# P read in place in 64-query blocks on TensorE column tiles, with V copied by halves, in a fused attention and gMLP block

## The chip, the cores and the metric

The kernel runs on one core of one Trainium2 chip. The metric is device time in microseconds (us); lower is better. A core has five engines with instruction queues of their own: TensorE (PE in the profile, with its weight loads listed apart as PEld), VectorE (DVE), ScalarE (ACT), GpSimd (POOL) and SyncE (SP), which issues most DMAs. Engines wait for each other through semaphores; within an engine instructions run in the order in which they were written.

## The reference

One token sequence of 2048 rows and 448 columns goes through two sub-blocks. Both are modulated by six vectors `mod = silu(c) @ w_mod`.

```python
h = layernorm(x) * (1 + ca) + sa
q, k, v = split(h @ wqkv)                      # 16 heads of 28
scores = q @ k.T * 28 ** -0.5
scores = where(0 <= i_query - i_key < 256, scores, -1e9)
x = x + ga * (softmax(scores) @ v) @ wo        # sliding window of 256

h = layernorm(x) * (1 + cb) + sb
z = gelu(h @ w_in)                             # 1792 columns
g = w_sp @ layernorm(z[:, 896:]) + b_sp        # w_sp mixes the 2048 rows
x = x + gb * (z[:, :896] * g) @ w_out
```

## The kernel before, in words

The rows are cut into 16 tiles of 128 and four blocks of 512. All work is entered as operations in a small planner (`Sched`, with one `add` for each). A long string, `ORDER`, lists operation numbers with the engine that takes each and the PSUM or SBUF slot that it gets: that string is the written order of every engine's queue. The semaphore waits follow from the dependencies. On an engine, an operation that waits holds up everything listed behind it.

*Head.* x, `w_mod`, and the query, key and value weights are loaded. The narrow products of `mod_cols` (L535, L540) turn c into the modulation columns; L540 writes a second copy into the upper 64 partitions, on the second column tile of the array. Statistics come from `stats` (L592 to L600), the normalised rows from `norm` (L609 to L620), the transposes from PE (L666) for the first two blocks and from DMA for the others. Q and K are projected by blocks of 512 rows (L696 for the first four groups of block 0, L708 for the others, L743 for the keys of the last block), V by tiles (L756), with 32 columns for each head: 28 values, a one that sums up P, and three unused (`Vaug`).

*Attention.* A query tile sees up to three key blocks of 128: the oldest (partly masked), the middle one (whole) and its own (partly masked). Each query tile is worked in two halves of eight heads. For tiles 0 and 1 L832 makes the scores. For tiles 2 to 15 L858 makes them with matmuls of 32 rows of the array (four heads side by side on four row tiles) into four PSUM banks, packed so that the oldest and the own block share columns: 36 matmuls for each half, the last 16 of them with 64 stationary columns on two column tiles. L867 adds the middle block of the other four heads by one product of 512 columns with a block-diagonal copy of Q (`QBD`, made by DMA at L734). ACT exponentiates 2048 and 512 columns (L819) into `PW`. DVE multiplies the packed part with the mask (L874, two products of 1024 columns for each half) and writes it, spread out again, into a second buffer `PT`. L901 is P·V: the stationary operand is a 128x128 block of P (128 keys, 128 queries), the moving operand 32 columns of `Vaug`; three key blocks and eight heads make 24 matmuls for each half. DVE divides by the sums (L915, L917), a DMA transposes the result (`oT`), L926 multiplies with `wo`, L931 adds x.

*Second half.* Statistics and a DMA transpose again (`hT2`), L951 modulates, L1011 and L1032 make z, ACT applies gelu (L1018, L1040), DVE normalises the second half of z (L592, L1023). L1055 is the spatial product (448 matmuls of 512 columns, with `w_sp` transposed by DMA), L1059 and L1062 add the bias and multiply, L1072 multiplies with `w_out`, L1082 adds x and SP writes the tile out.

The functions that the change touches and what calls them:

## Time and profile before

| | us |
|---|---|
| median of 3 runs | 280.3 (280.0 to 280.85) |
| the profiled execution's own time | 279.08 |
| its span, first to last instruction | 277.4 |

| engine | busy us | share of the span | instructions |
|---|---|---|---|
| PE | 266.4 | 96% | 3198 |
| PEld | 140.8 | 51% | 3225 |
| DVE | 164.4 | 59% | 364 |
| ACT | 128.2 | 46% | 154 |
| POOL | 127.2 | 46% | 191 |

The granted TensorE clock was 1.0 all through. The shares are means over stages of different kinds: in the attention stage DVE, ACT and PE are all close to full, in the last 118 us PE alone works and the others follow it. A matmul's length in the table includes its way through the array, and matmuls overlap: how fast they follow each other is read from their starts, not from their lengths. A row of the waits names who waited, for whom, the sum, the number of waits and the longest.

### The profile page before, as it was taken

How to read it: one execution, taken by the hardware profiler on the slowest of the kernel's cores; microseconds unless marked ns; L12 is line 12 of the kernel's file. 1: busy time of each engine (PE TensorE's matmuls, PEld its weight loads, DVE VectorE, ACT ScalarE, POOL GpSimd, SP SyncE). 2: the span in 40 equal slices, each digit the busy share in tenths (PEclk: the TensorE clock that was granted, in tenths of full speed). 3: DMA queues.
4: the chain of work that ended last, by engine and by line, in shares of the span. 5: the costliest groups of instructions: out<-in, count | busy, mean ns of one | idle time of the engine just before them, and what ended most of it. 6: DMA issues, size and time to landing. Idle time of an engine off the chain costs nothing.

```text
span 277.4 us, 7383 instructions
## 1 busy us (share of the span) xinstructions
PE 266.4 (96%) x3198; PEld 140.8 (51%) x3225; DVE 164.4 (59%) x364; ACT 128.2 (46%) x154; POOL 127.2 (46%) x191
## 2 busy tenths in 40 slices
PE   4999999999999999999999999999999999999995
PEld 1636466656576766444444444444444444444452
DVE  5679999989989999679798300300320042025434
ACT  2587999999999999577676600000000000000000
POOL 6831826914725669884949000600571065334110
PEclk9999999999999999999999999999999999999999
DMA  7966142145993666834999999100000000001113
GB/s 208 304 170 205 23 91 47 21 80 96 121 225 79 80 80 97 194 77 83 190 176 205 206 197 187 35 0 0 0 2 0 0 0 2 0 0 56 62 50 99
DMA packets 65843, 26.01 MB, mean 94 GB/s; under 512 B 56466, under 2 KB 64723, under 8 KB 65811
## 3 DMA queue, kind: packets, MB, share of 16 engines
q1 hardware_dynamic: 65168, 24.68, 43.4%
q10 hardware_dynamic: 642, 0.86, 1.1%
q8 instruction: 25, 0.41, 0.6%
q14 instruction: 8, 0.06, 0.1%
HBM read 9.01 MB, written 1.84 MB: 39 GB/s over the span
## 4 chain that ended last, share of the span: by engine, by line
PE 82%; DVE 8%; DMA 4%; POOL 3%; issue 1%; ACT 0%; ACTq 0%; SPq 0%; POOLq 0%
PE ps L1055 35%; PE ps L1032 8%; PE ps L1072 7%; PE ps L1011 6%; PE ps L708 5%; PE ps L901 5%; PE ps L858 3%; DMA hT<-xn 3%; PE ps L926 3%; PE ps L756 3%; PE ps L867 2%; DVE st_all L592 2%; PE ps L557 1%; DMA c_row<-in_c_dram 1%; PE ps L696 1%; POOL hT L951 1%
## 5 line engine op out<-in xcount | busy, mean ns | idle before, releaser
L819 ACT ACTIVATE PW<-ps 128x2048 bf16<-128x2048 f32 (+1 forms) x56 | 67.4, 1242 | 2.9 <-PE ps L867 1.1
L1059 DVE TENSOR_TENSOR tmpg<-ps,bsp_bc 128x512 bf16<-128x512 f32 x28 | 19.1, 691 | 83.4 <-PE ps L1055 69.3
L1062 POOL TENSOR_TENSOR z1T<-tmpg,z1T 128x512 bf16<-128x512 bf16 x28 | 31.9, 1153 | 79.3 <-DVE tmpg L1059 79.3
L1055 PE MATMUL ps<-wspB,z 128*128 128x512 bf16 x218 | 49.5, 379 | 0.3
L1055 PE MATMUL ps<-wspA,z 128*128 128x512 bf16 x220 | 48.8, 379 | 0.3 <-issue 0.2
L874 DVE TENSOR_TENSOR PT<-PW,mask 128x1024 bf16<-128x1024 bf16 x56 | 38.9, 721 | 0.7 <-ACT PW L819 0.7
L1055 PEld LDWEIGHTS ps<-wspA,z 128*128 128x128 bf16 x224 | 21.8, 98 | 26.6 <-issue 0.4
L1055 PEld LDWEIGHTS ps<-wspB,z 128*128 128x128 bf16 x224 | 21.9, 98 | 26.2
L600 POOL TENSOR_TENSOR rs_all<-ve_all,neghalf 128x1 f32<-128x1 f32 (+2 forms) x37 | 23.6, 645 | 3.7 <-DVE ve_all L597 3.0
L1011 PE MATMUL ps<-w_in,hT 64*128 64x448 bf16 x224 | 23.0, 349 | 1.2 <-DVE hT L951 0.6
L901 PE MATMUL ps<-Vaug,PT 128*128 128x32 bf16 x496 | 24.1, 177 | 0.1
L901 PEld LDWEIGHTS ps<-Vaug,PT 128*128 128x128 bf16 x496 | 21.8, 96 | 4.0 <-DVE PT L894 0.6
L1032 PE MATMUL ps<-hT,w_in 64*128 64x512 bf16 x196 | 22.5, 376 | 0.0
L1072 PE MATMUL ps<-w_out_g,z1T 128*128 128x448 bf16 x112 | 22.2, 352 | 0.0
L708 PE MATMUL ps<-hT,WQK 128*128 128x512 bf16 x80 | 20.5, 379 | 1.3 <-issue 0.4
L616 POOL TENSOR_SCALAR xn<-x_sb,rs_all,ve_all 128x448 bf16<-128x448 bf16 x21 | 18.1, 863 | 7.0 <-DMA hT<-xn 6.4
L901 PE MATMUL ps<-Vaug,PW 128*128 128x32 bf16 x224 | 20.1, 176 | 0.0
L592 DVE BATCH_NORM_STATS2 st_all<-x_sb 128x6 f32<-128x448 bf16 x32 | 18.9, 610 | 1.6 <-DMA x_sb<-in_A_x_dram 1.5
L592 DVE BATCH_NORM_STATS2 st_all<-z 128x6 f32<-128x448 bf16 x32 | 18.3, 607 | 1.7 <-ACT z L1018 1.7
L901 PEld LDWEIGHTS ps<-Vaug,PW 128*128 128x128 bf16 x224 | 17.6, 96 | 1.9
L597 POOL TENSOR_SCALAR ve_all<-mv_all 128x1 f32<-128x1 f32 (+2 forms) x20 | 6.6, 334 | 25.1 <-DVE mv_all L595 21.5
L1018 ACT ACTIVATE z<-ps 128x896 bf16<-128x896 f32 x16 | 14.1, 916 | 7.8 <-PE ps L1011 6.8
(101 smaller groups left out, 343.9 us busy)
## 6 DMA issues: line engine op xcount, KB each, us to landing
out_dram<-fin SPq DMA_DIRECT2D x16, 112.0 KB, 1.7
x_sb<-in_A_x_dram SPq DMA_DIRECT2D x3, 448.0 KB, 3.9
wmod<-in_w_mod_dram SPq DMA_DIRECT2D x1, 1344.0 KB, 9.5
w_in<-in_B_w_in_dram SPq DMA_DIRECT2D x1, 1344.0 KB, 8.2
QBD<-qT SPq DMA_DIRECT2D x16, 64.0 KB, 2.5
w_out_g<-in_B_w_out_dram SPq DMA_DIRECT2D x1, 784.0 KB, 4.9
bsp_bc<-in_B_b_sp_dram SPq DMA_DIRECT2D x1, 512.0 KB, 5.0
x_sb<-in_A_x_dram SPq DMA_DIRECT2D x2, 224.0 KB, 4.2
```

The source lines that it names most:

```text
L592: st = [dve(0.62 if True else 0, lambda e, t=t, ci=ci, s=s: e.bn_stats(st_all[:, slot, t, ci, :], s()), deps(t), prio) for ci, s in enumer ...
L600: rs = pool(0.53 + 0.15 * len(tiles), lambda e: e.tensor_tensor(rs_all[:, slot, a:b], ve_all[:, slot, a:b], neghalf[:, 0:b - a], ALU.pow), ...
L708: m = pe(4 * MMS, [lambda e, h=h, g=g, kc=kc, tb=tb: e.matmul(ps[:, h.slot[0], :], lhsT=WQK[:, kc, 4 * g:4 * g + 4, :].rearrange("p a b -> ...
L819: ex = act(xdur, lambda e, out_ap=out_ap, in_ap=in_ap: e.activation(out_ap(), in_ap(), ACT.Exp, scale=SCALE), [s], v - 8.0 + u, takes, tab ...
L874: return dve(0.70, lambda e: e.tensor_tensor(cols(hp.slot[0] * 2048 + 1024 * k, [[256, 4], [128, 2], [1, 128]]), cols(at_w() + 128 + 192 * ...
L901: fns.append(lambda e, hp=hp, hO=hO, hi=hi, bi=bi, kb=kb, hd=hd, nb=nb, a=at[hi][bi], p_of=p_of: e.matmul(ps[:, hO.slot[0], 32 * hd:32 * h ...
L1011: return lambda e, kc, p0, start, stop: e.matmul(ps[:, hs[t % 2].slot[hf], 0:D], lhsT=hT[p0:p0 + 64, kc, t * 128:(t + 1) * 128], rhs=w_in[ ...
L1032: return lambda e, kc, p0, start, stop: e.matmul(ps[:, hs[b // 2].slot[b % 2], :], lhsT=w_in[p0:p0 + 64, kc, ft * 128:(ft + 1) * 128], rhs ...
L1055: m = pe(16 * MMS, [lambda e, h=h, si=si, ft=ft, tb=tb: e.matmul(ps[:, h.slot[0], :], lhsT=z2[:, si, ft * 128:(ft + 1) * 128], rhs=(wspA i ...
L1059: a = dve(0.7, lambda e, h=h, ht=ht, tb=tb: e.tensor_tensor(tmpg[:, ht.slot[0], :], ps[:, h.slot[0], :], bsp_bc[:, tb * 512:(tb + 1) * 512 ...
L1062: u = pool(1.16, lambda e, ht=ht, ft=ft, tb=tb: e.tensor_tensor(z1T[tb][:, ft, :], tmpg[:, ht.slot[0], :], z1T[tb][:, ft, :], ALU.mult), [ ...
L1072: return [lambda e, ft=ft: e.matmul(ps[:, h.slot[0], 0:D], lhsT=z1T[t // 4][:, ft, (t % 4) * 128:(t % 4 + 1) * 128], rhs=w_out_g[:, ft, :] ...
```

## The change

- **P·V.** P stays where the exponential wrote it (`PW`). For each head there are six products in place of three: the stationary operand is 64 queries wide, and the products of the first and of the last 64 queries go to the two column tiles of the array (`tile_position=(0, 0)` and `(0, 64)`). The packed columns now hold, in one 128-key column block, keys of the own block beside keys of the oldest, so V must be packed alike: `VX` holds four versions of V (two of them with the other half of the keys zero), made by two copies and four DMAs for each block of four tiles (`V_half`, `vdma` below); `VX` has two buffers and its zeros are set early.
- **Scores.** 40 matmuls for each half, all with 64 stationary columns (32x64 tiles), laid out for the new packing.
- **Mask.** One product in place, of 1024 columns, for eight heads; `mask3` is made by eight small copies. `PT` is left to tiles 0 and 1, at the place of `w_in`, whose loads now wait for the P·V of these tiles.
- **Head.** x, `w_mod` and the query and key weights are asked for in another order and from other queues, the projection weights only after x has landed; the first projection groups are query 0, key 0, query 1, key 1; the modulation columns of the first half drop the second copy (L540).
- **Second half.** Every other tile's layer norm of z takes its sums on ACT (the gelu's accumulator and a square) in place of DVE statistics; the scale and shift of four others go to POOL. The last output tile is worked in two column halves.
- **`ORDER`** is written anew: 1127 operations in place of 1155.

```diff
 ORDER = """
-2.a 24.v 33.g 0.s 25.v 26.v 27.v 36.g 37.g 3.a 1.s 34.g 4.a 31.g 28.v 5.s 35.g 8.a 29.v 38.g 6.s 9.a 7.s 43.a 39.g 53.p.1 54.p.2 55.p.3 44.p.0 130.v
...
+1.a 24.v 35.g 0.s 25.v 26.v 27.v 38.g 39.g 2.a 4.s 36.g 3.a 33.g 28.v 5.s 29.v 30.v 37.g 56.a 31.v 40.g 41.g 6.s 7.s 8.s 9.s 143.v 66.p.1 67.p.2
...
-    t_mA = pe(1.2, mod_cols(hA, (0, 1), True), [t_wmA, t_sc, t_p2], -60.0, [hA])
+    t_mA = pe(0.92, mod_cols(hA, (0, 1), False), [t_wmA, t_sc, t_p2, t_p2b], -60.0, [hA])
...
+            first = (0, 4, 1, 5)
+            hq = {g: Hold(bA) for g in first}
...
+        a, b = (2, 4) if tb == 0 else (4 * tb, 4 * tb + 4)
+        vx = lambda k, p0, p1, tb=tb, a=a, b=b: VX[p0:p1, tb % 2, k, a % 4:a % 4 + b - a].rearrange("p j c -> p (j c)")
+        vo = lambda p0, p1, a, b: Vaug[p0:p1, a:b].rearrange("p t h d -> p (t h d)")
+        v = 40.0 * tb - 46.0
+        for k, p0, q0, back in ((0, 0, 64, 0), (3, 64, 0, 2)):
+            need = [t_va, [V_ready[t] for t in range(a - back, b - back)]]
+            same = add({"dve": (0.1 + 0.16 * (b - a), lambda e, k=k, p0=p0, vx=vx, vo=vo, a=a - back, b=b - back: e.tensor_copy(vx(k, p0, p0 + 64), vo(p0, p0 + 64, a, b))),
+                        "pool": (0.1 + 0.57 * (b - a), lambda e, k=k, vx=vx, vo=vo, a=a - back, b=b - back: e.tensor_copy(vx(k, 0, 128), vo(0, 128, a, b)))}, need, v)
+            V_half.setdefault(tb, []).append(same)
+            other = a - 2 if back == 0 else a
+            for n, (k2, to, of, first) in enumerate(((k, q0, p0, other), (2 - k // 3, p0, p0, a - back))):
+                name = "d_v%d%d%d" % (tb, k, n)
+                dsem.append(name)
+                V_half[tb].append(add({"sp": (0.6, lambda e, vx=vx, vo=vo, k2=k2, to=to, of=of, first=first, n=b - a: e.dma_start(
+                    vx(k2, to, to + 64), vo(of, of + 64, first, first + n)))}, [t_va, [V_ready[t] for t in range(first, first + b - a)], t_vz[tb % 2] if n else same], v,
+                    dma=name, lat=0.34 * (b - a), tail=2.1))
...
-                for place in (((0, m, 128, 0, 128, 0, 0),), ((k, o, 128, 0, 64, 128, 0) for k in range(2)), ((k, n, 128, 64, 128, 256, 0) for k in range(2)),
-                              ((k, *e) for k in range(2) for e in ((n, 64, 0, 64, 192, 0), (o + 64, 64, 64, 128, 192, 64)))):
...
+                for k in range(2):
+                    for key, lo, hi, col, p0 in ((n, 0, 128, 0, 0), (o + 64, 0, 128, 64, 64), (o, 0, 64, 0, 64), (n + 64, 64, 128, 128, 0)):
                         for t in range(4):
...
+                for p0 in (0, 64):
+                    for t in range(4):
...
-                mks = [mask_all(k) for k in range(2)]
...
+                fk = lambda e, at_w=at_w, cols=cols: e.tensor_tensor(
+                    cols(at_w(), [[512, 4], [128, 4], [1, 64]], PW), cols(at_w(), [[512, 4], [128, 4], [1, 64]], PW),
+                    cols(0, [[0, 4], [64, 4], [1, 64]], mask3), ALU.mult)
+                mk = add({"dve": (0.73, fk)}, [exs[0]] + t_mk3, v - 7.0)
...
+                    return [(Vaug[:, kbs[1]], mid(0), 0, 64), (Vaug[:, kbs[1]], mid(1), 64, 64), (vx(0), at(0), 0, 64), (vx(3), at(128), 64, 64),
+                            (vx(1), at(64), 0, 64), (vx(2), at(64), 64, 64)]
...
+                            ps[q0:q0 + w, hO.slot[0], 32 * hd:32 * hd + 32], lhsT=of(hi), rhs=V[:, hd, :],
+                            start=first, stop=last, **(dict(tile_position=(0, q0)) if w == 64 else {})))
...
+    for d in t_win_l:
+        d.deps.update(all_PV[:4])
...
+    BY_POOL = (0, 4, 8, 12)
+    BY_ACT = (1, 3, 5, 7, 9, 11, 13, 15)
...
+            q = act(1.1, lambda e, t=t, less=less, square=square, hj=hj: e.activation(
+                fin[:, 2 * hj.slot[0]:2 * hj.slot[0] + 2, :].rearrange("p a d -> p (a d)"), z2[:, t, :], ACT.Square, bias=less, accum_out=square), [a], v, [hj])
...
+            for c0, c1 in ((0, D // 2), (D // 2, D)) if t == NT - 1 else ((0, D),):
```

## The prediction, made before the change was run

> **What bounds the kernel now.** I first read the busy table by stretches, cut at three events of the chain: the first windowed score block (29.46), the last P·V product (112.12) and the first spatial product (156.59). The first row and the last two are out of one answer; the second is an answer of its own.

> ```profile
> 112.12:156.59 44.47, 43.36 (x418) 20.15 (x414) 36.20 (x99) 29.85 (x45) 29.66 (x58) 1.00 0.84 159
> 156.59:274.45 117.86, 117.35 (x550) 54.58 (x558) 27.80 (x43) 2.28 (x5) 32.86 (x29) 1.00 0.20 44
> ...
> 12.87:29.46 16.59, 15.85 (x166) 8.46 (x167) 14.02 (x37) 13.56 (x18) 6.36 (x12) 1.00 0.60 177
> ```
> ```profile
> 29.46:112.12 82.66, 80.90 (x2002) 52.65 (x2015) 78.17 (x161) 78.32 (x80) 48.56 (x68) 1.00 0.52 89
> ```

> Columns: the stretch and its length, then busy us (and instructions) of PE, PEld, DVE, ACT, POOL, the clock, DMA. In the attention stage, 82.66 us long, three engines are nearly full: PE 80.90, ACT 78.32, DVE 78.17. Behind it DVE and ACT have room and PE has none. A busy PE may still be waiting inside its pipeline, so the decisive view is the table of waits of PE alone, cut to the same stretch; beside it the loader's, whose first row is the largest:

> ```profile
> PE ps L708 <- issue: 0.4, 2, 0.2
> PE ps L1011 <- ACT PW L819: 0.3, 1, 0.3
> PE ps L708 <- DVE rec_all L915: 0.2, 1, 0.2
> ```
> ```profile
> PEld ps L858 <- ACT PW L819: 6.1, 16, 0.5
> ```

> PE waited 0.9 us in 82.66. The loader waited 6.1 us for the exponentials, but under matmuls that still streamed. **So the attention stage lasts as long as PE's own instructions**, and so do the stages behind it. DVE and ACT are merely close. An edit is worth what it takes from or adds to PE's instruction stream.

> **The change part by part.** First PE's prices per half of a query tile (eight heads), 28 halves with the three-block window. The rows, from the timeline of PE in narrow windows (start, length, line, form):

> ```profile
> 81.05 0.18 PE L901 MATMUL ps<-Vaug,PT 128*128 128x32 bf16 x1
> 81.16 0.55 PE L858 MATMUL ps<-qT,KT 32*128 32x128 bf16 x36
> 81.64 1.07 PE L743 MATMUL ps<-hT,WQK 128*128 128x128 bf16 x16
> ...
> 87.42 0.19 PE L901 MATMUL ps<-Vaug,PT 128*128 128x32 bf16 x1
> ...
> 88.64 0.38 PE L867 MATMUL ps<-QBD,KT 128*128 128x512 bf16 x1
> ```
> ```profile
> 25.76 0.17 PE L535 MATMUL ps<-sc_sb,wmod 128*64 128x1 bf16 x1
> 25.77 0.17 PE L540 MATMUL ps<-sc_sb,wmod 128*64 128x1 bf16 x1
> 25.79 0.17 PE L535 MATMUL ps<-sc_sb,wmod 128*64 128x1 bf16 x1
> 25.80 0.17 PE L540 MATMUL ps<-sc_sb,wmod 128*64 128x1 bf16 x1
> 25.82 0.17 PE L535 MATMUL ps<-sc_sb,wmod 128*64 128x1 bf16 x1
> 25.84 0.17 PE L540 MATMUL ps<-sc_sb,wmod 128*64 128x1 bf16 x1
> ```
> ```profile
> 57.81 0.35 PE L858 MATMUL ps<-qT,KT 32*128 32x128 bf16 x20
> ```
> ```profile
> 58.09 0.15 PEld L858 LDWEIGHTS ps<-qT,KT 32*64 32x64 bf16 x16
> 58.29 0.10 PEld L867 LDWEIGHTS ps<-QBD,KT 128*128 128x128 bf16 x1
> ```

> *P·V.* Today 48 products with the full array run from 87.42 to 88.64: 25 ns each, 24 per half, 0.61 us. The change issues 48 per half, each with 64 queries stationary, alternating between the two column tiles. The trace has this form once: L535 and L540 alternate between column tiles with 64 stationary columns. Over the five steps from 25.76 to 25.84 that is 0.08/5, 16 ns each, so 48 cost 0.75 us: **+0.14 us per half, +4 us in 28**. Those rows move 1 column, the new ones 32. The bounds are 13 ns, the 32 columns at the 512-column pace (2.37 us for 11 L1055 products, so 0.42 ns a column) with nothing else (0.64), and 32 ns without overlap between tiles (1.54).

> ```profile
> 239.94 2.37 PE ps L1055 x11
> ```

> *Scores.* Today's 36 matmuls take 81.16 to 81.64, 0.48 us, with the way out (below). Inside, the array changes from 128 to 64 stationary columns: the twentieth matmul of the block starts about 57.97 (57.81 + 0.35, less its own 0.19), and the loads of the 64-column form only at 58.09, about 0.09 later than the pace. The change uses the 64-column form throughout: 40 matmuls in five rounds of eight tiles, of 128, 64, 128, 64 and 128 moving columns, 512 together. Paced by columns alone that is 0.22, with the start of a round 0.24. From above: today's two rounds of 64 columns last from 58.09 to 58.29 with the way out, so 0.06 a round; five, and 0.027 more for each that moves 128 columns, make 0.37. I take 0.30, between the ends, since the trace has no third such round. Against 0.48 − 0.09 = 0.39 that is **−0.09 per half, −2.5 us**, bounds −4.2 and −0.6.

> *Changes of the array's shape.* Between the last L901 at 81.05 and L858 at 81.16 lie 0.11 us where 0.025 would do: 0.09 for each change. P·V today has the full shape, as the projections have, and needs none. On column tiles it has a shape of its own. I counted both strings of the written order from the first windowed score block to the last P·V product: 57 changes today, 80 after. **23 × 0.09 = +2.1 us**, between 0 (hidden by loads ahead) and 2.1.

> *Sum on PE:* +4.0 − 2.5 + 2.1 = **+3.6 us**. With all three at their low ends it is +0.8 − 4.2 + 0 = −3.4, with all at their high ends, as long as the tiles overlap, +4.0 − 0.6 + 2.1 = +5.5.

> *DVE.* The mask product (L874) goes from two per half to one of the same 1024 columns:

> ```profile
> L874 DVE TENSOR_TENSOR PT<-PW,mask 128x1024 bf16<-128x1024 bf16 x56 | 38.9, 721 | 0.7 <-ACT PW L819 0.7
> L894 DVE TENSOR_TENSOR PT<-PT,mask 128x512 bf16<-128x512 bf16 x8 | 3.8, 499 | 0.0
> ```

> That takes off 28 × 0.72 = 20 us; the first two tiles save about 1; eight mask copies and five V copies come back (0.4 to 0.7 each by such rows, 3 to 6 us). About 15 us leave an engine that PE does not wait for: **0 on the path**. In place P also ends the PT buffers, which nobody waited for.

> *ACT.* The exponentials stay 28 × (2048 + 512 columns), and the orders leave ACT 22 evictions of some 0.6 in the stage against 23. 0, hidden under PE.

> *V copies.* Per block of four tiles two copies (8, three of them on POOL) and four DMAs (16) fill the halves; the first P·V of a block now also waits for them. Nearest row, a transfer of the same kind:

> ```profile
> QBD<-qT SPq DMA_DIRECT2D x16, 64.0 KB, 2.5
> ```

> Eviction 0.6, copy 0.4 to 2.4, four issues with transposes between them some 5, landing 2.5: 8 to 11 us. Between the last V of a block and the P·V that needs it the new order puts some 11 us of PE work (tiles 4, 8, 12) or 14 (tile 2). Just covered: 0, but behind a late P·V stand all later PE instructions. SP also carries the transposes to which these DMAs are added, and the first w_in load now waits for the P·V of tiles 0 and 1, ahead of oT.0 and the next QBD copies on SP; those have some 10 us too.

> *Head.* The first scores wait for a key eviction today:

> ```profile
> 18.68 0.29 PE L832 MATMUL ps<-qT,KT 32*128 32x128 bf16 x8 [0.69 <-ACT KT L718]
> ```

> With projection groups 0, 4, 1, 5 first, two more groups cover that: −0.7. Eight narrow products fewer in mA: −0.2. Against it the query and key weights are asked for only after x has landed, the key weights are needed before the first product, and 5.8 to 6.5 us went from issue to landing of these; 0 to +1. Together −0.5.

> *Second half.* Eight layer norms move from DVE statistics to a square on ACT: ACT has 29.85 of 44.47 us, and eight passes over 896 columns of about 1 us make 38 to 39. DVE loses 11. PE stays the bound: 0. The last-listed output is whole in both orders, so splitting tile 15 changes nothing at the end: 0.

> **Total** +3.6 − 0.5 = +3.1 on the profiled execution's 279.08 us (span 277.4 and 1.7 around it) gives 282.2. That execution lies 1.2 under the median 280.3 of the three runs; for the median I say **283.3**.

> **The rivals.**
> *Loads bind (faster).* If the loader's 6.1 us behind L819 were real waiting, a lighter DVE would end evictions sooner and free the banks: −6.1 + 3.1 gives 277.3. For it: 16 such waits. Against it: PE's own 0.9 us, and L819 itself does not get shorter. 0.12.

> *The rounds flow (no change).* Scores at 0.24 (−4.2) with half of the shape changes hidden (+1.0) and P·V +4.0, head −0.5: +0.3, 280.6. 0.13.

> *New waits (slower still).* The V copies or the squares on ACT come late; decided when the chain copy, SP, landing exceeds 11 us. Three blocks at 1 to 2 us each: +3 to +5 on the forecast, 286 to 288. 0.13.

> *The column tiles do not overlap at 32 moving columns.* 48 × 0.032 = 1.54 us per half, +0.93 × 28 = 26 instead of 4: 305. The rows of L535 and L540 speak against it. [...] 0.04.

> **How the numbers follow.** The forecast, slower by PE's added instructions, has 0.58, with 281 to 286 as its own range. One measurement of this kernel can tell about 0.3% (0.8 us) from no change. Slower: 0.58 + 0.13 + 0.04 = 0.75; same 0.13; faster 0.12. The range 280.0 to 287.5 leaves out the faster rival, all three low ends at once, the 305 and part of the new waits.

> **What would show it.** Right: the attention stage is some 3 us longer with PE still waiting about 1 us in it; L874's successor has 28 instructions near 0.72; P·V 48 in about 0.75 us; DVE falls well under PE. Score blocks of 0.24 or of 0.37 move the time by −1.7 or +2. Wrong: the stage gets shorter (then PE was not the bound), or PE waits for V's DMAs or, behind it, for ACT.

## The result, and the profile after

The changed kernel takes 295.75 us (median of 4 runs, 292.48 to 298.9), the kernel before 280.15 us (279.57 to 280.85) on the same chip: a ratio of 1.0487 (95% interval 1.0439 to 1.0535), slower by 13.6 us by the ratio and by 15.6 by the medians. The ratio leaves out runs at the upper end, so it lies below the quotient of the two medians, 1.056. The forecast was 283.3 us, in a range of 280.0 to 287.5: the sign was right, the size far off. The profiled execution took 294.49 us, span 292.7.

First the same stages as in the prediction, with the cuts at the same events (first windowed score block, last P·V product, first spatial product), from the table by stretches of the kernel after:

```profile
11.16:27.94 16.78, 16.05 (x177) 8.51 (x177) 12.71 (x38) 12.59 (x18) 5.03 (x8) 1.00 0.64 206
27.94:127.83 99.89, 91.41 (x2769) 59.92 (x2779) 76.05 (x173) 79.80 (x79) 36.85 (x57) 0.97 0.65 118
127.83:171.35 43.52, 43.52 (x427) 20.66 (x426) 26.67 (x79) 34.49 (x65) 28.79 (x56) 1.00 0.78 137
```

The attention stage is 99.89 us long, before 82.66: +17.2. The stage before it ends 1.5 us earlier, the one behind it is 0.9 us shorter (44.47 before), and the last one 0.5 longer. So the whole loss is in the attention stage. DVE and ACT are no longer near full there, but for the greater part because the stage got longer: their sums, 76.05 and 79.80 us, were 78.17 and 78.32 before. PE, whose stage this is, is idle for 8.5 of the 99.89 us (before 1.8 of 82.66), and the mean of its clock fell to 0.97.

What it waited for, from the table of waits of PE (who, for whom, us in total, times, longest):

```profile
PE ps L942 <- issue: 3.7, 4, 2.0
...
PE ps L899 <- issue: 1.5, 2, 1.1
PE ps L781 <- DVE KT L744: 1.5, 1, 1.5
PE ps L733 <- issue: 0.6, 4, 0.2
PE ps L733 <- DVE KT L744: 0.5, 1, 0.5
```

L942 is P·V, L899 the scores, L781 and L733 projections. There is no wait for a V transfer and none for ACT of any size. The largest name is "issue": PE waited for nothing that the profile shows, and still did nothing. The chain that ended last shows where, in order of time:

```profile
102.25 0.31 PE ps L899 x32
102.56 0.18 PE ps L905 x8
102.74 0.77 PE ps L942 x41
103.51 1.99 issue
105.49 0.27 PE ps L942 x7
105.77 0.32 PE ps L914
106.09 0.89 PE ps L768 x16
106.98 0.47 PE ps L899 x23
```

P·V stops after 41 of its 48 products, stands for 2 us, and then does the last 7. Nothing begins or ends at that point in the program: the 42nd product reads the same columns of P as the 41st, writes the same bank, and has no wait of its own. There are six such stops in the stage. I counted PE's records (loads, matmuls and its few event instructions) from the start of the program, and set beside each stop the last packet of the queue that carries instructions:

```
record  at 256k +  stop from, us    packet landed   PE resumes   resumes after landing
4020    180        91.29  0.58      90.37           91.87        1.50
4276    180        96.24  0.46      95.21           96.70        1.49
4532    180       100.60  0.74     100.01          101.34        1.33
4788    180       103.32  2.17     104.18          105.49        1.31
5812    180       120.88  1.31     120.72          122.18        1.46
6068    180       126.66  1.07     126.42          127.73        1.32
```

The stops stand at exact steps of 256 records, and each ends 1.3 to 1.5 us after a packet of instructions has landed. They are 6.3 us together, taken from start to start (5.2 us in the waits, which count from the modelled end of the product ahead). The packets are these, before in the first fence and after in the second (queue, packets, MB):

```profile
q8 instruction: 25, 0.41, 0.6%
```
```profile
PE 276.8 (95%) x3990; PEld 148.6 (51%) x4013; DVE 151.7 (52%) x360; ACT 135.9 (46%) x176; POOL 111.1 (38%) x166
...
PEclk9999999999999987999999999999999999999999
...
q8 instruction: 31, 0.51, 0.8%
...
L942 PE MATMUL ps<-VX,PW 128*64 128x32 bf16 x896 | 25.6, 185 | 3.7 <-issue 3.7
...
L919 DVE TENSOR_TENSOR PW<-PW,mask 128x1024 bf16<-128x1024 bf16 x28 | 22.0, 797 | 2.6 <-ACT PW L857 2.4
```

0.51 MB in 31 packets is 16.4 KB each. PE's 8,054 records hold 31 full blocks of 256, its 6,461 of before 25: one packet for each block in both traces, which makes 64 B for a record. So **PE's instructions come in blocks of 256, and in the changed kernel a block is sometimes used up before the next is there**: six times in this stage, for 0.46 to 2.17 us.

How short a block may be can be estimated from the same rows. In the attention stage the load of the next block mostly starts 0.4 to 1.4 us after PE enters a block, takes 0.9 to 1.7 us, and where PE stood waiting it went on 1.3 to 1.5 us after the landing: by this estimate 2.6 to 4.6 us in all. At 49 instructions per us a block lasts 5.2 us, at 59 it lasts 4.3, so a late load shows.

The digits 8 and 7 in the clock's row are a second loss. The stretches show it (PEclk is the third number from the end):

```profile
98.00:105.00 7.00, 4.97 (x191) 3.79 (x190) 5.34 (x15) 5.03 (x5) 1.11 (x2) 1.00 0.92 120
105.00:112.00 7.00, 6.51 (x165) 5.00 (x165) 3.17 (x7) 2.96 (x3) 0.55 (x3) 0.64 0.21 42
```

From 106.9 us, behind the longest stop, the clock is 0.5 for 6.83 us, which costs 3.4 at most. The four runs stand in the order of their mean clock: 292.48 us at 0.994, 294.49 at 0.988, 297.02 at 0.983, 298.9 at 0.977. By these means they had about 3.5, 7, 10 and 14 us at half clock; half of the difference, 5 us, is most of the 6.4 between the first and the last.

### The profile page after: what moved, and what is told of

Same layout as the page of the kernel before. It is cut to its first block, busy times and chain, and to the rows that moved or that the text cites. A ratio compares the mean times of both kernels' runs of the same rounds, so it can differ in the third digit from the quotient of the medians.

```text
span 292.7 us, 8997 instructions
## 1 busy us (share of the span) xinstructions
PE 276.8 (95%) x3990; PEld 148.6 (51%) x4013; DVE 151.7 (52%) x360; ACT 135.9 (46%) x176; POOL 111.1 (38%) x166
## 4 chain that ended last, share of the span: by engine, by line
PE 85%; DVE 7%; issue 3%; ACT 2%; DMA 1%; POOL 0%; ACTq 0%
PE ps L1128 33%; PE ps L942 8%; PE ps L1059 7%; PE ps L1147 7%; PE ps L1105 7%; PE ps L733 5%; PE ps L967 4%; PE ps L781 3%; PE ps L899 3%; PE ps L914 2%; ACT PW L857 1%; PE ps L905 1%; PE ps L768 1%; PE ps L575 1%; PE ps L719 1%
## 5 line engine op out<-in xcount | busy, mean ns | idle before, releaser
L942 PE MATMUL ps<-VX,PW 128*64 128x32 bf16 x896 | 25.6, 185 | 3.7 <-issue 3.7
L942 PEld LDWEIGHTS ps<-Vaug,PW 128*64 128x64 bf16 x448 | 22.8, 116 | 7.7 <-issue 4.7
L942 PE MATMUL ps<-Vaug,PW 128*64 128x32 bf16 x448 | 25.2, 187 | 0.0
L942 PEld LDWEIGHTS ps<-VX,PW 128*64 128x64 bf16 x896 | 23.7, 116 | 1.0 <-issue 1.0
L919 DVE TENSOR_TENSOR PW<-PW,mask 128x1024 bf16<-128x1024 bf16 x28 | 22.0, 797 | 2.6 <-ACT PW L857 2.4
L733 PE MATMUL ps<-hT,WQK 128*128 128x512 bf16 x85 | 21.7, 380 | 1.5 <-issue 0.6
L1147 PE MATMUL ps<-w_out_g,z1T 128*128 128x448 bf16 (+1 forms) x119 | 22.0, 341 | 0.0
L1147 PEld LDWEIGHTS ps<-w_out_g,z1T 128*128 128x128 bf16 x119 | 11.6, 98 | 9.9
L1157 DVE TENSOR_TENSOR fin<-ps,x_sb 128x448 bf16<-128x448 f32 (+1 forms) x17 | 9.8, 594 | 12.2 <-PE ps L1147 10.3
L1113 ACT ACTIVATE z1T<-ps 128x512 bf16<-128x512 f32 x28 | 14.5, 609 | 3.1 <-PE ps L1105 3.1
L1059 PEld LDWEIGHTS ps<-w_in,hT 64*128 64x128 bf16 x224 | 10.7, 94 | 10.4 <-ACT z L1082 0.4
```

Source lines behind the costliest of these rows:

```text
L733: m = pe(4 * MMS, [lambda e, h=h, g=g, kc=kc, tb=tb: e.matmul(ps[:, h.slot[0], :], lhsT=WQK[:, kc, 4 * g:4 * g + 4, :].rearrange("p a b -> ...
L919: fk = lambda e, at_w=at_w, cols=cols: e.tensor_tensor(cols(at_w(), [[512, 4], [128, 4], [1, 64]], PW), cols(at_w(), [[512, 4], [128, 4], ...
L942: (more if w == 64 else fns).append(lambda e, hO=hO, hi=hi, hd=hd, V=V, of=of, q0=q0, w=w, first=bi < (2 if nb == 3 else 1), last=bi >= le ...
L1059: return lambda e, kc, p0, start, stop: e.matmul(ps[:, hs[t % 2].slot[hf], 0:D], lhsT=hT[p0:p0 + 64, kc, t * 128:(t + 1) * 128], rhs=w_in[ ...
L1147: return [lambda e, ft=ft: e.matmul(ps[:, h.slot[0], c0:c1], lhsT=z1T[t // 4][:, ft, (t % 4) * 128:(t % 4 + 1) * 128], rhs=w_out_g[:, ft, ...
```

## The experiments

The theories. **Supply**: PE takes 59 instructions per us in this stage where it took 49, and blocks run out. **Array work**: P·V, scores and shape changes are simply longer than I priced, and the stops are a detail. **V copies**: the new copies and transfers made the loss, by waits or by keeping the DMA engines busy. The table has every run; "stops" are those over 0.38 us at a step of 256 in the profile's attention stage, and instructions per us are PE's records from 29 us to the last P·V, with the stops taken out. Stops and clock are those of one execution each, and they vary from one execution to the next.

| kernel | median us | ratio to before (95%) | stops, us | at half clock, us | instructions per us |
|---|---|---|---|---|---|
| before | 280.15 | 1 | 0 | 0 | 49 |
| after | 295.75 | 1.0487 (1.0439–1.0535) | 6: 6.3 | 6.8 | 59 |
| e1_cols_in_before | 290.5 | 1.0373 (1.0322–1.0424) | 2: 2.3 | 0 | 59 |
| e2_nops_in_before | 376.97 | 1.3455 (1.3384–1.3526) | – | 112.6 | 30 |
| e3_no_v_transfers | 292.33 | 1.0458 (1.0379–1.0536) | 3: 3.8 | 3.4 | 60 |
| e4_no_zero_halves | 283.74 | 1.0132 (1.0060–1.0204) | 2: 2.4 | 3.4 | 53 |
| e5_nops_for_zero_halves | 350.13 | 1.2477 (1.2403–1.2552) | – | 68.3 | 36 |
| e7_blanks_early | 295.38 | 1.0551 (1.0480–1.0622) | 5: 7.1 | 10.2 | 58 |
| e8_traffic_in_before | 283.98 | 1.0101 (1.0057–1.0145) | 1: 1.3 | 0 | 47 |
| e9_cols_and_traffic | 292.75 | 1.0464 (1.0375–1.0552) | 4: 3.8 | 3.4 | 58 |
| e10_no_halves_no_transfers | 281.91 | 1.0088 (1.0058–1.0119) | 3: 1.8 | 0 | 55 |
| e12_longer_not_denser | 286.67 | 1.0247 (1.0200–1.0294) | 2: 0.9 | 0 | 52 |
| e15_changed_and_longer | 296.67 | 1.0600 (1.0548–1.0652) | 5: 5.3 | 3.4 | 58 |

The ten kernels with stops have 33 of them, and each ends 1.2 to 1.6 us after a packet of instructions has landed.

**Column tiles alone, in the kernel before.**

> The kernel before, with nothing changed but its P.V product: each of its 24 matmuls of a half becomes two on the column tiles 0 and 64, with the same V. It adds 1,440 matmuls and loads to TensorE's stream in the attention stage, no V copies, no transfers and no order of its own. Supply theory (TensorE's instructions come in blocks of 256, and a block that is used up in less than about 4 us waits for the next): P.V 48 in about 0.75 us instead of 0.61, 2 to 5 us of TensorE work with the changes of array shape, and beside it stops of 0.3 to 2 us at every 256th instruction: 286 to 294 us. Array-work theory (only the column tiles' own price): 282 to 285 us, no stop at a step of 256. V-copies theory (waits and traffic of the new copies and transfers made the loss): 282 to 285 us as well, no stop.

```diff
-                        fns.append(lambda e, ...: e.matmul(
-                            ps[:, hO.slot[0], 32 * hd:32 * hd + 32], lhsT=p_of(a), rhs=Vaug[:, kb, hd, :],
+                        for q0 in (0, 64):
+                            fns.append(lambda e, ..., q0=q0: e.matmul(
+                                ps[q0:q0 + 64, hO.slot[0], 32 * hd:32 * hd + 32], lhsT=p_of(a)[:, q0:q0 + 64], rhs=Vaug[:, kb, hd, :],
```

290.5 us, 1.0373: by the ratios three quarters of the changed kernel's loss, without a V copy, a transfer or a new order. The chain of this kernel has two stops, at records 5056 and 5312, again 256 apart, in the middle of score blocks:

```profile
107.67 0.47 PE ps L858 x32
108.13 1.01 issue
109.15 0.22 PE ps L858 x4
109.37 0.48 PE ps L902 x24
109.85 1.00 PE ps L743 x16
110.85 0.86 PE ps L902 x48
111.72 0.32 PE ps L867
112.04 0.48 PE ps L858 x35
112.52 0.91 issue
```

The rest, some 8 us, is array work in an order that was written for another product: 48 products cost 0.86 with the way back to the full array (L902 x48), where 24 cost 0.61; groups of 24 cost 0.48 against 0.30, and here nearly every group pays for a change of shape on both sides. The trace has 109 changes in the stage where the kernel before has 55: 54 × 0.09 = 4.9 us, beside 28 × 0.15 = 4.2 for the products. Supply's range holds the time and its stops came; but it had put 2 to 5 us on array work, so that the range holds is in part luck. The theory of array work was wrong here on both counts: it expected no stop, and 282 to 285.

**Fewer products.**

> The changed kernel without the two P.V products against the half-blank V copies 1 and 2: 32 matmuls of a half instead of 48, so a part of P.V is left out; all copies, transfers and the order stay. Supply theory: 896 fewer instructions (3.5 blocks); the array work falls by 16 x 16 ns x 28 = 7 us, and most of the 6 us of stops and the 3.4 us at half clock go too: 280 to 285 us. Array-work theory: 7 us less, 288 to 289 us. V-copies theory: the stops stay, 288 to 289 us.

```diff
-                    return [..., (vx(0), at(0), 0, 64), (vx(3), at(128), 64, 64),
-                            (vx(1), at(64), 0, 64), (vx(2), at(64), 64, 64)]
+                    return [..., (vx(0), at(0), 0, 64), (vx(3), at(128), 64, 64)]
```

283.74 us, 0.6 to 2.0% over the kernel before: by the ratios 3.55 points less than the changed kernel, 9.9 us, by the medians 12.0; the work taken out is 28 × 0.25 = 7.1 us (a half's P·V takes 0.61 where it took 0.865, start to start). So 3 to 5 us more went than the work. The stops fell from 6.3 to 2.4 us and the half clock from 6.8 to 3.4. One long stop is left, on L914:

```profile
PE ps L914 <- issue: 1.9, 1, 1.9
```

**Empty instructions.**

> The kernel before with two empty instructions (no-ops, which the array never sees) ahead of each matmul of P.V: the same 1,440 more instructions in TensorE's stream as the kernel with column tiles in before has, without any more array work. Supply theory: P.V still about 0.61 us where no block ends, but stops appear at steps of 256 instructions: 283 to 290 us. Array-work theory and V-copies theory: as before, 280 to 281 us. If the sequencer itself is the slow part (it needs time for each empty instruction), P.V gets longer everywhere, evenly, and no stop stands out.

> The same, with two empty instructions in the place of each matmul left out, so that TensorE's stream is as long as in the changed kernel and the array work 7 us less. Supply theory: the stops at steps of 256 stay or grow, since each block is used up sooner: 289 to 297 us, well above the kernel without the empty instructions. Array-work theory and V-copies theory: the same time as the kernel without the empty instructions, within 1 us.

```diff
+                        fns += [lambda e: e.nop(hint="p", nofuse=True), lambda e: e.nop(hint="p", nofuse=True)]
                         fns.append(lambda e, ...: e.matmul(
```

The edit is that of the first; the second has the same two in the place of each product left out. Both missed the three theories: 377 and 350 us. What came is the last case of the first expectation, for which it gave no time: each empty instruction takes time of its own. The timeline of PE in the first of them, where the no-ops set the pace (at full clock):

```profile
92.40 0.18 PE L902 MATMUL ps<-Vaug,PW 128*128 128x32 bf16 x1
92.56 0.35 PE L902 MATMUL ps<-Vaug,PT 128*128 128x32 bf16 x2
92.89 0.18 PE L902 MATMUL ps<-Vaug,PW 128*128 128x32 bf16 x1
```

Products come 0.165 us apart instead of 0.025, so a no-op costs about 70 ns: (0.165 − 0.025)/2. Over the run it is (376.97 − 280.83)/1,440 = 67 ns, with 112.6 us at half clock in it. At 30 instructions per us a block lasts 8.5 us, no stop stands out, and the two kernels say nothing on supply. They were the wrong tool, and the question was put again with real work (below).

**As much work, fewer instructions.** This is the test that the no-ops should have been.

> The changed kernel without those two products (part of P.V is left out) and with the 128x512 score product against QBD issued twice (the second gives the same values): 16 matmuls of 16 ns go from each half and one of 0.215 us comes, 30 instructions fewer. The array work is that of the changed kernel less 1 us (28 x 0.215 = 6.0 in, 7.1 out). Supply theory: a stream with fewer instructions per us has few stops, so the 6.0 us come in full at most, on 283.7: 287 to 290 us. Array-work theory (the loss is the length of the work): 294 to 295.5 us, near the changed kernel.

```diff
-                unit(EPRI, MMS, [lambda e, ...: e.matmul(
+                unit(EPRI, MMS, 2 * [lambda e, ...: e.matmul(
```

286.67 us, ratio 1.0247: just under what supply expected, and 9 us under the changed kernel (6.7 by the ratios), though the array has only 1.1 us less to do. Against the kernel without the added product 3.2 us came of 6.0. PE's waits for instructions are nearly gone:

```profile
PE ps L905 <- issue: 0.3, 1, 0.3
PE ps L899 <- issue: 0.2, 1, 0.2
```

**More work, the same instructions.**

> The changed kernel with that same product issued twice, and nothing left out: 28 x 0.215 = 6.0 us more of array work, and 2 instructions more of a half. Supply theory: each block of 256 lasts longer (about 0.3 us), so the stops shrink and part of the added work replaces them: 297 to 300 us. Array-work theory: 6.0 us longer, 301 to 302.5 us.

296.67 us, just under supply's range and well under the other. The second issue adds 6.0 us of matmul; the time grows by 0.9 us by the medians and by 3.2 by the ratios (1.0600 against 1.0487, each interval some 3 us wide), in either case by less than the work. The stops went from 6.3 to 5.3 us, the half clock from 6.8 to 3.4; one stop is as long as any:

```profile
PE ps L967 <- issue: 2.2, 1, 2.2
PE ps L942 <- issue: 1.5, 3, 0.6
...
PE ps L905 <- issue: 0.5, 1, 0.5
```

The two together, the first above all, settle the first question: what is lost beyond the work itself goes with instructions per us, and not with the array's time.

**Transfers.** The load of a block goes through the same DMA engines as everything else (the page of the changed kernel puts its queue, q8, at 0.8% of the 16 engines' time, and the queue of the data, q1, at 49.0%). In the trace of the changed kernel it starts 0.4 to 1.4 us after PE enters a block in 13 of 22 blocks; but it starts 2.0 to 3.2 us after (a stop not counted) in four of the five blocks in whose first 4 us the DMA engines are over 90% busy. One more came 2.6 us after with the engines some 0.7 busy. So the V transfers could delay it.

> The changed kernel with its 16 V transfers cut to 32 of up to 2,048 columns each, so that the half copies hold wrong values; the copies by engines, TensorE's stream, the waits and the written order stay. Traffic theory (the stops come where the load of the next block of 256 instructions starts late, because the transfers have the DMA engines full): most of the 6 us of stops at steps of 256 and the half-clock stretch of 3.4 us go: 285 to 289 us. Density theory (the blocks are used up too fast whatever the DMA engines do): the stops stay, 293 to 296 us. V-copies theory (TensorE waits for the copies themselves): the same as the density theory, as the waits on semaphores were under 1 us.

```diff
-                    vx(k2, to, to + 64), vo(of, of + 64, first, first + n))
+                    vx(k2, to, to + 64)[:, 0:32], vo(of, of + 64, first, first + n)[:, 0:32])
```

VectorE's copies are also twice as tall here, 128 partitions in place of 64; they take as long (0.66 us, 0.69 in the changed kernel).

292.33 us: between the two expectations. By the ratios it is 0.8 us faster than the changed kernel, by the medians 3.4, and the ratios' intervals overlap. In the profile three stops of 1.2 to 1.35 us are left of six, 3.8 us of 6.3. A fourth, of 0.85 us on L905, also ends 1.5 us after a packet but stands three records behind a step of 256; it is not in the table, and with it 4.7 us are left. PE's waits:

```profile
PE ps L942 <- issue: 2.2, 2, 1.2
...
PE ps L899 <- issue: 1.0, 1, 1.0
...
PE ps L905 <- issue: 0.6, 1, 0.6
```

> The kernel before with 16 transfers more from SBUF to SBUF, of 112 and 224 KB, at about the times and in the number of the changed kernel's V transfers (from wv into room that nothing reads). Traffic and density together (a block must be used up fast and its successor come late): before's blocks last 4.2 us and more, so hardly a stop: 280 to 283 us. Traffic alone: stops of several us as in the changed kernel, 285 to 290 us. Density alone: 280 to 281 us.

> The kernel before with P.V on column tiles, and the same 16 transfers more. With the column tiles alone it took 290.5 us, with 2.3 us of stops. Traffic and density together: more and longer stops, 4 to 8 us of them, 293 to 298 us. Density alone: 290 to 291.5 us. Traffic alone: as much more here as the transfers cost in the kernel before.

```diff
+    dums = []
+    for tb in range(NB4):
+        n = 2 if tb == 0 else 4
+        for k, (at, to, of) in enumerate(((dum, 64, 0), (dum, 0, 0), (fin, 0, 64), (fin, 64, 64))):
+            ...
+            dums.append(add({"sp": (0.6, lambda e, ...: e.dma_start(
+                at[to:to + 64, 0:n]..., wv[of:of + 64, 0:n]...))}, ...))
```

The `w_out` load and the last outputs also wait for these transfers. In the kernel before they cost 2.8 us by the ratio (1.6 to 4.1), inside what both together were to give, while the median lies 1 us above it. But it is hardly by stops: one of 1.3 us, and beside it waits for other transfers that now came later, which the kernel before did not have:

```profile
PE ps L868 <- DMA QBD<-qT: 1.1, 1, 1.1
PE ps L927 <- DMA hT<-o_sb: 1.0, 1, 1.0
```

On the column tiles they raise the stops from 2 to 4 (2.3 to 3.8 us), and the ratio from 1.0373 to 1.0464, with intervals that overlap; the time is just below what I expected of both together.

> The changed kernel without the two products against the half-blank copies (part of P.V is left out) and with its V transfers cut to 32 columns (the half copies hold wrong values). Left out alone, the products took it to 283.7 us and the transfers to 292.3 us. If stops at steps of 256 instructions come from the two together (blocks used up fast, and their successors held up by full DMA engines), there is hardly a stop left: 279.5 to 282 us. If the transfers cost something of their own that has nothing to do with the stops, the 3.4 us come off in full: about 280 us, but the stops are as in the kernel without the products (2.4 us in that profile). If the transfers do nothing where the stream is short: 283 to 284 us.

281.91 us, at the upper end of the first case: by the ratios 1.2 us less than with the transfers, again inside the intervals. Three short stops are left. So the transfers add 0.8 to 2.8 us by the ratios in the four pairs, part of it by later blocks; only the pair on the kernel before is beyond its interval. They are the smaller part. How much of a late block is due to traffic stays open: with the V transfers cut there is still a load that starts 3.6 us behind the entry into a block, a stop not counted.

**The head.**

> The changed kernel with two of GpSimd's blanks (of QBD and of VX, 0.95 us each, at 36.6 to 38.5 us) moved ahead into its idle stretch at 28.4 us; all else stays. Theory for the 2.3 us that TensorE loses at 34.75 and 38.83 us: VectorE's normalisation and mask product, which took 1.49 and 1.50 us beside those blanks instead of 0.39 and 0.70, kept it waiting; the two take their usual times then, the wait at 38.8 shrinks from 1.5 us to under 0.5, and the kernel is 1 to 2 us faster, 293.5 to 295 us. Rival: the order of VectorE's evictions alone makes the wait, and nothing changes, 295 to 296 us.

In the written order, the two words that blank the second buffers of QBD and VX stand behind GpSimd's V copy:

```diff
-201.g ... 271.g ... 63.g 54.g
+201.g 63.g 54.g ... 271.g
```

295.38 us: no gain to be seen, though 1 us would hardly stand out from runs that spread over 3. Moving the blanks moved the collision. VectorE and GpSimd in this kernel:

```profile
28.88 1.34 DVE L509 COPY mask<-mask 64x64 bf16<-64x64 bf16 x1
...
38.86 1.52 DVE L919 TENSOR_TENSOR PW<-PW,mask 128x1024 bf16<-128x1024 bf16 x1
```
```profile
28.35 0.95 POOL L536 MEMSET QBD<- 128x1024 f32 x1
29.23 0.95 POOL L516 MEMSET VX<- 128x1024 f32 x1
...
37.77 2.07 POOL L594 TENSOR_TENSOR wo_g<-wo_g,gg_sb 128x448 bf16<-128x448 bf16 x2
```

A copy of 64x64, which took 0.11 to 0.18 us in the changed kernel, took 1.34 beside the blanks in their new place; the mask product still took 1.52, now beside the products for wo_g. PE's wait at the later place fell from 1.5 to 0.7 us, and a new one of 0.8 came at the earlier:

```profile
PE ps L733 <- DVE modT L567: 0.8, 1, 0.8
PE ps L781 <- DVE KT L744: 0.7, 1, 0.7
```

The sum is the same, so the expected time failed. The reason stands, as far as these rows go: the passes that were long stood beside GpSimd's, in the old place and in the new. That the order of the evictions alone makes the wait is out, since the wait moved with the blanks.

## Why the prediction was wrong

The step that failed is the one on which all else was built: **"the attention stage lasts as long as PE's own instructions … An edit is worth what it takes from or adds to PE's instruction stream."** That held for the kernel before, with 49 instructions per us. I then added 1,450 instructions to that stage and priced each by the time it takes in the array. That they also have to arrive was not among the terms, the rivals or the signs. The row of the queue of instructions stood in the page that I read. By the profile it is 6.3 us of stops and up to 3.4 us of half clock, of +15.4 (294.49 against 279.08); the prediction had 0 for it.

The other steps, against the trace of the changed kernel:

- *P·V, +4.0.* Right. The chain has 96 products in 1.63 us with the way back to the full array:

```profile
88.07 0.31 PE ps L899 x32
88.38 0.18 PE ps L905 x8
88.56 1.63 PE ps L942 x96
```

  With 0.11 for the way back that is 15.8 ns each, 0.76 for 48 (I said 0.75), +4.2 in all. The column tiles do overlap, so that rival is out.
- *Scores, −2.5.* Mis-sized. L899 and L905 in the same rows make 0.49 for the 40 matmuls, before 0.48; without the way out 0.40, where I took 0.30 and had 0.37 as the upper bound (its terms, 5 × 0.06 and 3 × 0.027, make 0.38). The saving is nothing, and 28 × 0.01 comes on top: 2.8 us more on the sum.
- *Shape changes, +2.1.* The price holds: from start to start L914 takes 0.31 ahead of a score block and 0.216 ahead of a projection, so 0.09 for the change into another shape; the way back behind P·V is 0.11.
- *DVE and ACT, 0.* Right on the path. But the 15 us that were to leave VectorE did not leave the stage, where its sum fell by 2.1 us. The masks gave back 16.9 (38.9 us before, 28 × 0.797 = 22.0 after), and other work came in, among it 9 evictions of V where 4 stood (+3.2), more normalisations (+3.0) and statistics (+2.4), and the V copies (3.1).
- *V copies, 0.* Right as far as waits go: PE never waited for one. Wrong by a way that I did not list: their traffic costs 0.8 to 2.8 us in the pairs above, with one pair of four beyond its interval. That it makes other transfers late is shown; that the instructions are among them is only argued, from when their loads start.
- *Head, −0.5.* The first windowed scores are 1.5 us earlier, but two waits of PE for VectorE's evictions behind them (0.88 and 1.83 us from start to start, where the usual step is 0.21) cost 2.3: +0.8.
- *Second half, 0.* Right: −0.9 and +0.5 us in the two stages behind.

Put together, 4.2 + 0.3 (scores) + 2.1 + 0.8 − 0.9 + 0.5 = 7.0 us for work and edges, and 9.7 for stops and clock, make 16.7 where 15.4 were found; the shape changes and the half clock stand at their full price in it. The kernel with as much work and fewer instructions gives the same from the other side: 7.0 us over the kernel before, with 0.9 of stops in it and 1.1 less work, so 7.2. With the failed step mended, the rest of my errors would have come to 3.9 us, 287.2, still inside the range. (My own sum on the median, 280.3 + 3.1, is 283.4; I wrote 283.3.)

## What to carry to other kernels

Ahead of a change that trades few large matmuls for many small ones, count the instructions per us that the engine will need (in blocks of 256), and compare that with what the kernel already sustains: here 49 per us ran without a stop (47 with the added transfers had one of 1.3 us), 52 to 55 had 0.9 to 2.4 us of stops, and 58 to 60 had 2.3 to 7.1. Where a profile names "issue" in the middle of a group of like matmuls, look at the step between such stops (here 256 records) before looking at operands; and where the instructions are what is short, long matmuls put between cost less than their own time (here 0.9 to 3.2 us of 6.0).
